# Column-softmax products with the operands exchanged, and a transpose by DMA behind them

## The chip, the cores and the metric

The kernel runs on one core of a Trainium2 chip. A core has five instruction streams that work side by side and meet only through semaphores: TensorE (PE, matrix products, with a separate weight-load part PEld), VectorE (DVE), ScalarE (ACT), GpSimd (POOL) and SyncE (SP), which in this kernel issues DMAs and computes nothing. Each stream takes its instructions strictly in the order in which the program lists them; an instruction that waits holds back all that stand behind it on the same stream. The metric is the device time of one execution in microseconds (us); lower is better.

## The reference, cut to what matters

```python
B, H, S, Ns, D = (8, 8, 512, 32, 64)
scores = scale * x @ state.T                 # per (batch, head): 512 x 32
a = softmax(scores, -1);   xread = a @ state # row softmax, result 512 x 64
scores2 = scale * state @ x.T                # per (batch, head): 32 x 512
a2 = softmax(scores2, -1); sread = a2 @ x    # column softmax, result 32 x 64
attn = concatenate([xread, sread], axis=2)   # per head 544 rows of 64
t = attn.transpose(0, 2, 1, 3).reshape(B * 544, 512)
h = maximum(t @ w_in, 0)                     # 512 -> 2048
out = (s * h * h + b) @ w_out                # 2048 -> 512
```

The change concerns `sread`: for each batch and head, the 32 x 512 weights `a2` times the 512 x 64 block of `x`. The 8 x 32 rows of `sread` (all heads side by side, 512 columns) are the last 256 tokens that go through the two layers.

## The kernel before, in words

The order of all the work is written out by hand in the list `ORDER` (lines 15 to 79). Each word names a piece and its arguments; the loop at line 785 calls the pieces one after another, and each engine's stream is the order of these calls. Batches are handled in the order 0 to 7 for the main work, while the `sread` work of a batch comes later and in the order 3, 4, 5, 2, 6, 0, 7, 1.

For one batch `b` the `sread` work is this chain. `nm`, `E2` and `a2` make the column softmax on ACT and DVE (tile `a2`, 128 partitions = 4 heads x 32 states, two groups `g` of 4 heads, 512 tokens). `tr` (line 446) turns it by one DMA issued from SP into `a2T`, with tokens on the partitions: 8 blocks of 128 x 128. `V` (line 450) multiplies it on PE with `xn`, the batch's `x` with tokens on the partitions, and `srd` (line 470) copies the result `vps` from PSUM into `srdT` on ACT.

In `V` of the kernel before, `xn` (64 columns, the head's D) is the operand that is loaded into the array, and 32 columns of `a2T` move through it. The result has D on the partitions, 64 for each of two heads, so the array is used as two column tiles of 64. For each `k` (four pairs of heads) and each of `SCH` = 4 chunks of tokens there are two matmuls: 32 per batch. The result is already in the layout that the first layer wants, and `srd` writes it with a step: `srdT` is `[P, NK, Ns, B]` and `srdT[:, :, :, b]` touches every eighth fp16 element, 16 bytes apart.

`lsr` (line 544) is the first layer for the `sread` tokens: 16 calls of four matmuls each, all of which read `srdT` as the moving operand with 256 columns (32 states x 8 batches). For each `k` those 256 elements lie next to one another. They need `srdT` of all eight batches; the first call (`lsr.14`) stands near the end of `ORDER`.

The main work of a batch: `M` makes the product of states and `w_in`, `Mc` copies it from PSUM, `l` (line 526) is the first layer, `s` squares, `S` makes sums of blocks, and `P` (line 645) is the second layer by seven block products. The products go into PSUM banks X, Y and W; DVE takes a bank out with `ev` (line 660) into the output tiles `osx0` and `osx1`. Bank W is read out twice, by `ev.b.W1` after its first block product and by `ev.b.W2` after its second, which adds on top; so the second product into W (`P.b.10` and `P.b.11`) may only start when `ev.b.W1` has read the bank. `put.b.i.rr` (line 668) stores 128 rows of `osx{i}` by two DMAs, from SP for all batches but the last.

`osx0` and `osx1` have one buffer each (`bufs=1`, line 614). So the first `ev` of the next batch into the tile waits until all four store DMAs of the batch before have landed: `ev.b.X1` waits for the stores of `put.(b-1).0.*`, `ev.b.W1` for those of `put.(b-1).1.*`.

The SP stream therefore carries, mixed in one order: the transposes `tr` (line 448) and `xt` (line 316, 16 blocks of 128 x 128, `x` with D on the partitions), the copies of line 275, and the stores.

Of the kernel before, what the change touches and what calls it, by code (L numbers as in the profile page):

```python
# [11 lines left out]
FP16 = mybir.dt.float16  # L12
# [70 lines left out]
def kernel(  # L83
# [12 lines left out]
    nc = tc.nc  # L96
# [4 lines left out]
    B, H, S, D = x.shape  # L101
    Ns = state.shape[2]
    DM = H * D
    DF = moe_w_in.shape[1]
    P = 128
    NK = DM // P
    NKF = DF // P
    NG = H // 4
    SCH = S // P
# [10 lines left out]
    konst = ctx.enter_context(tc.tile_pool(name="konst", bufs=1))  # L120
    wpool = ctx.enter_context(tc.tile_pool(name="wpool", bufs=1))
    xpool = ctx.enter_context(tc.tile_pool(name="xpool", bufs=4))
    apool = ctx.enter_context(tc.tile_pool(name="apool", bufs=1))
# [11 lines left out]
    def two_banks(name, dtype=FP32, own=False):  # L135

        pool, tag = (ps_t, "pt") if own else (ps_a, "pa")
        return pool.tile([P, 2, 2048 // mybir.dt.size(dtype)], dtype, name=name, tag=tag)

    def mm(out, lhsT, rhs, start=True, stop=True, tp=None, is_transpose=None, skip=False):  # L140
        skip = skip or out.offset * mybir.dt.size(out.dtype) >= 2048
        return nc.tensor.matmul(  # L142
            out, lhsT, rhs, start=start, stop=stop, tile_position=tp,
            is_transpose=is_transpose, skip_group_check=skip,
        )
# [27 lines left out]
    ones16 = konst.tile([P, 512], FP16, name="ones16")  # L173
    c16 = konst.tile([P, DM], FP16, name="c16")
    bias_bc = konst.tile([P, DM], FP32, name="bias_bc")
    srdT = konst.tile([P, NK, Ns, B], FP16, name="srdT")
    w_in16 = [wpool.tile([P, NK, 512], FP16, name=f"w_in16_{j}") for j in range(NJ)]
    w_out16 = wpool.tile([P, NKF, DM], FP16, name="w_out16")

# [58 lines left out]
    def w_in_f(k, f):  # L238
        return w_in16[f // 4][:, k, P * (f % 4) : P * (f % 4) + P]
# [41 lines left out]
    at = [dict() for _ in range(B)]  # L281

    def sm(b, key, shape, dtype, pool=None, bufs=None):
        if key not in at[b]:
            at[b][key] = (pool or smpool).tile(
                shape, dtype, name=f"{key}_{b}", tag=key, bufs=bufs
            )
        return at[b][key]
# [161 lines left out]
    def at_V(own, *bs):  # L450

        pair = two_banks(f"vps_{bs[0]}", own=own)
        for v, b in enumerate(bs):
            vps = pair[:, v, : NK * Ns].rearrange("p (k n) -> p k n", n=Ns)
            a2T, xn = at[b]["a2T"], xn_t[b]
            for k in range(NK):
                for i in range(SCH):
                    for g in range(NG):
                        hp = k ^ 2 * g
                        mm(  # L460
                            vps[D * g : D * g + D, k, :],
                            xn[:, 4 * g + k, i, :],
                            a2T[:, SCH * g + i, Ns * hp : Ns * hp + Ns],
                            start=(i == 0),
                            stop=(i == SCH - 1),
                            tp=(0, D * g),
                        )
            at[b]["vps"] = vps

    def at_srd(b):  # L470
        nc.scalar.copy(srdT[:, :, :, b], at[b]["vps"])

    def at_M(b, j, own):
        M = sm(b, "M", [P, NG, DF], FP16, mpool)
# [26 lines left out]
    def in_turn(shape, name, tag, n):  # L501
        k = turns[tag] = turns.get(tag, -1) + 1
        return rpool.tile(shape, FP16, name=name, tag=f"{tag}{k % n}", bufs=1)

    def layer1(tag, f, terms, ntok):
        hps = ps_h.tile([P, ntok], FP32, name=f"hps_{tag}_{f}", tag="ph")
        for i, (lhsT, rhs) in enumerate(terms):
            to = hps if len(rhs.shape) == 2 else hps.rearrange("p (c q) -> p c q", c=2)
            nc.tensor.matmul(to, lhsT, rhs, start=(i == 0), stop=(i == len(terms) - 1))  # L509
        q, i = f // 4, f % 4  # L510
        if (tag, q) not in R_t:
            R_t[tag, q] = in_turn([P, 4, ntok], f"r_{tag}_{q}", "r", 3)
        nc.scalar.activation(R_t[tag, q][:, i], hps, AF.Relu)  # L513
# [12 lines left out]
    def layer1_x(b, f):  # L526
        M, A = at[b]["M"], at[b]["A"]
        layer1(b, f, [(M[:, g, P * f : P * f + P], of_head(b, A, g)) for g in range(NG)], S)
# [13 lines left out]
        squared(e, new_G(b, S)[:, f : f + 2, HALF * p : HALF * p + HALF], R_t.pop((b, f, p)))  # L542

    def layer1_sr(f):
        layer1("sr", f, [(w_in_f(k, f), srdT[:, k].rearrange("p n b -> p (n b)")) for k in range(NK)], B * Ns)

    ops_t, visits = {}, {}

# [215 lines left out]
    def evict_sr(i, n, bank, plus, last):  # L764
# [12 lines left out]
        "sb": spread_scalars, "xT": at_xT, "xt": at_xt, "cs": copy_states, "T": at_T, "keep": at_keep, "U": at_U, "mu": at_mu, "D": at_D,  # L777
        "E1": at_E1, "z": at_z, "At": at_At, "A": at_A, "nm": at_nm, "nms": at_nms, "E2": at_E2, "a2": at_a2,
        "tr": at_tr, "V": at_V, "srd": at_srd, "M": at_M, "Mc": at_Mc,
        "lh": layer1_half, "sh": square_half, "l": layer1_x, "s": square, "lsr": layer1_sr,  # L780
        "ssr": lambda f, n, e: square("sr", f, n, e), "L": layer2, "out": out_x, "cps": bias_sum, "c": bias_c16,
        "bias": bias_all, "wsum": weight_sum, "S": act_sum, "P": product, "ev": evict, "put": put,
# [36 lines left out]
```

## Time and profile before

| what | value |
|---|---|
| median of 3 runs (lowest, highest) | 211.52 us (211.32, 211.72) |
| the profiled execution: its own time | 211.45 us |
| its span on the core | 209.7 us |
| PE busy | 200.1 us, 95% of the span |
| DVE / ACT / POOL busy | 179.0 us (85%) / 169.1 us (81%) / 47.4 us (23%) |
| granted TensorE clock, mean | 0.984 |
| HBM read / written | 20.48 MB / 8.91 MB |

The profiled execution lies inside the spread of the timed runs. Its time is 1.75 us above its span; that part lies outside what the trace shows.

How to read the rows in this document. A timeline row gives the start in us, the duration in us, the engine, the line of the kernel, the operation, what is written from what, the shape, and how many instructions were merged (`x32`). For PE the shape ahead of the result's is the loaded operand: `128*64` is 128 rows and 64 columns of the array. `SPq` is SP's queue: a row there is the time that the issue of a DMA takes, and the transfer itself goes on behind it. A group row of one line or one tile gives the least, the median and the greatest duration in ns and the first and last start; "DMA to landing" is the time from the start of an issue to the data's arrival. A row of stretches gives for each engine its busy time (and the instructions), then the granted clock, the DMA share and GB/s.

### The profile page before, as it was taken

The page shows a single profiled execution, that of the slowest core. Times are in us where ns is not written, and L with a number is a line of the kernel's source. Part 1 is how long each engine was busy: PE and PEld are TensorE (multiplying, and loading weights), DVE is VectorE, ACT ScalarE, POOL GpSimd, SP SyncE. Part 2 cuts the span into 40 slices and gives each one's busy share as a digit, 9 for nine tenths or more (in the row PEclk, how much of TensorE's full clock was granted, in tenths as well). Part 3 has the DMA queues.
Part 4 walks back from the last instruction along what each step waited for, and adds up shares of the span by engine and source line. Part 5 has one row for each costly group of instructions (what it writes and reads, how often), then busy time and mean ns, then how long its engine had stood idle before and what let it go on. Part 6 is the DMA issues. An engine that isn't in the chain of part 4 may idle for free.

```text
span 209.7 us, 4807 instructions
## 1 busy us (share of the span) xinstructions
PE 200.1 (95%) x1939; PEld 131.4 (63%) x1939; DVE 179.0 (85%) x276; ACT 169.1 (81%) x275; POOL 47.4 (23%) x63
## 2 busy tenths in 40 slices
PE   7498998999999999999999999999999999999992
PEld 2134343344576757676677677766777677888881
DVE  2998999799999899999999999999995984476571
ACT  4589999999999999989999677997989688634500
POOL 8553360524074009300470007100000000000000
PEclk9859999999999999999999999999999999999999
DMA  6999999699448539959799353719004910440055
GB/s 152 179 207 207 195 205 204 110 144 165 99 79 96 107 78 183 147 86 195 163 128 189 74 118 65 100 42 199 12 0 88 187 31 0 96 107 0 5 149 152
DMA packets 42475, 24.87 MB, mean 119 GB/s; under 512 B 24532, under 2 KB 37588, under 8 KB 42452
## 3 DMA queue, kind: packets, MB, share of 16 engines
q0 software_dynamic: 15408, 9.90, 34.0%
q1 hardware_dynamic: 25760, 13.70, 31.3%
q10 hardware_dynamic: 1284, 0.95, 1.6%
q8 instruction: 15, 0.25, 0.5%
q14 instruction: 8, 0.07, 0.1%
HBM read 20.48 MB, written 8.91 MB: 140 GB/s over the span
## 4 chain that ended last, share of the span: by engine, by line
PE 86%; DVE 6%; DMA 3%; ACT 1%; POOL 1%; issue 1%; DVEq 0%; POOLq 0%
PE opf_X L142 24%; PE hps L509 23%; PE opf_W L142 12%; PE opf_Y L142 6%; PE ops L558 5%; PE mps L142 4%; DMA w_in<-in_moe_w_in_dram 3%; PE hps_sr L509 3%; PE vps L142 2%; PE ops_sr_X L142 2%; DVE M L157 1%; PE hph L142 1%; ACT M L157 1%; PE dps L733 1%; PE ops_sr_W L142 1%; DVE g L519 1%
## 5 line engine op out<-in xcount | busy, mean ns | idle before, releaser
L513 ACT ACTIVATE r<-hps 128x512 f16<-128x512 f32 x120 | 69.2, 619 | 11.1 <-PE hps L509 9.0
L142 PEld LDWEIGHTS <-g 128*128 128x128 f16 x672 | 65.2, 98 | 17.8 <-issue 1.5
L509 PE MATMUL hps<-A,M 128*128 128x512 f16 x240 | 64.8, 379 | 0.4 <-ACT M L157 0.3
L517 ACT ACTIVATE g<-r 128x1024 f16<-128x1024 f16 (+1 forms) x37 | 46.1, 1262 | 0.0
L509 PEld LDWEIGHTS <-M 128*128 128x128 f16 x240 | 22.0, 98 | 19.7 <-issue 5.2
L142 PE MATMUL opf_X<-w_T,g 128*128 128x256 f16 x224 | 28.4, 273 | 0.0
L634 DVE TENSOR_TENSOR g<-g 128x1024 f16<-128x1024 f16 (+1 forms) x36 | 25.5, 709 | 0.6
L157 ACT CAST M<-mps 128x1024 f16<-128x1024 f32 x21 | 21.2, 1032 | 2.5 <-PE mps L142 2.5
L196 POOL DMA_DIRECT2D xn<-in_x_dram x32 | 18.5, 584 | 4.2 <-DMA w_in<-in_moe_w_in_dram 1.8
L634 POOL TENSOR_TENSOR g<-g 128x1024 f16<-128x1024 f16 x4 | 8.5, 2125 | 46.1 <-DVE g L634 32.4
L664 DVE SCALAR_TENSOR_TENSOR osx<-opf_X,sb_bc,bias_bc 128x512 f32<-128x512 f32 x21 | 15.5, 737 | 1.5 <-PE opf_X L142 1.4
L558 PE MATMUL ops<-w_out,g 128*128 128x512 f16 x64 | 16.0, 379 | 0.0
L142 PE MATMUL opf_X<-w_out,g 128*128 128x256 f16 x112 | 14.4, 273 | 0.0
L142 PE MATMUL opf_Y<-w_out,g 128*128 128x256 f16 x112 | 14.3, 273 | 0.0
L142 PE MATMUL opf_W<-w_T,g 128*128 128x256 f16 x112 | 14.2, 273 | 0.0
L142 PE MATMUL opf_X<-w_T,S 128*128 128x256 f16 x112 | 14.2, 272 | 0.0
L142 PE MATMUL opf_W<-w_out,g 128*128 128x256 f16 x112 | 13.9, 273 | 0.0
L142 PE MATMUL mps<-w_in,stT 64*32 64x512 f16 x256 | 12.4, 411 | 1.4 <-DMA w_in<-in_moe_w_in_dram 1.4
L157 DVE CAST M<-mps 128x1024 f16<-128x1024 f32 x11 | 13.2, 1215 | 0.4 <-PE mps L142 0.4
L513 ACT ACTIVATE r_sr<-hps_sr 128x256 f16<-128x256 f32 x16 | 6.1, 382 | 9.2 <-PE hps_sr L509 8.5
L142 PEld LDWEIGHTS <-S 128*128 128x128 f16 x112 | 11.0, 98 | 2.9 <-issue 0.2
L634 DVE TENSOR_TENSOR S<-g 128x1024 f16<-128x1024 f16 x14 | 9.5, 682 | 2.3 <-ACT g L517 2.2
(98 smaller groups left out, 272.9 us busy)
## 6 DMA issues: line engine op xcount, KB each, us to landing
out_dram<-osx SPq DMA_DIRECT2D x52, 128.0 KB, 2.4
xn<-in_x_dram POOLq DMA_DIRECT2D x32, 128.0 KB, 5.3
w_in<-in_moe_w_in_dram POOLq DMA_DIRECT2D x8, 256.0 KB, 9.4
w_out<-in_moe_w_out_dram POOLq DMA_DIRECT2D x4, 512.0 KB, 13.2
xh<-in_x_dram POOLq DMA_DIRECT2D x4, 256.0 KB, 11.3
out_dram<-osb SPq DMA_DIRECT2D x16, 64.0 KB, 1.8
xf<-in_x_dram SPq DMA_DIRECT2D x2, 256.0 KB, 3.6
out_dram<-osx ACTq DMA_DIRECT2D x4, 128.0 KB, 2.9
```

Of the source, the lines that this page charges most:

```text
L142: return nc.tensor.matmul(out, lhsT, rhs, start=start, stop=stop, tile_position=tp, is_transpose=is_transpose, skip_group_check=skip,)
L157: (engine.copy if engine is nc.scalar else engine.tensor_copy)(out, in_)
L196: nc.gpsimd.dma_start(out=xn_t[b][32 * jh : 32 * jh + 32].rearrange("t h c d -> t h (c d)"), in_=x[b].rearrange("h (t jh c) d -> jh t h (c ...
L509: nc.tensor.matmul(to, lhsT, rhs, start=(i == 0), stop=(i == len(terms) - 1))
L513: nc.scalar.activation(R_t[tag, q][:, i], hps, AF.Relu)
L517: nc.scalar.activation(g, r, AF.Square)
L519: e.tensor_mul(g, r, r)
L558: nc.tensor.matmul(ops_t[tag, rr], G_t[tag][:, f, P * rr : P * rr + P], w_out_f(f), start=(v == 1 and f == 4 * q), stop=(v == NKF // 4 and ...
L634: e.tensor_tensor(out, x, y, op)
L664: nc.vector.scalar_tensor_tensor(out, fast(b, name[0]), s_bc, out if plus else bias, ALU.mult, ALU.add)
L733: nc.tensor.matmul(dps, ones16[:, :P], ones16, start=True, stop=True)
```

## The change

Three things change.

`V`: the operands are exchanged. The 32 columns of `a2T` are loaded and 64 columns of `xn` move. The result has the states on the partitions, 32 for each of four heads, so the array is used as four column tiles of 32. There are still 32 matmuls per batch; the loop runs over `g`, then the chunks, then the four tiles `k`.

`srd`: ACT copies the 128 x 128 result into a new small tile `sr16` (two buffers), with neighbouring elements, and a DMA issued from SP transposes that into `srdT`. This is one more DMA per batch on SP's stream, of one 128 x 128 block, eight in all, and each waits for ACT's copy. The words of `ORDER` are the same; the new DMA stands where the word `srd.b` stands.

`srdT` becomes `[P, B, P]`: for each batch 128 columns, which are four groups `k` of 32 states. `lsr` reads `srdT[:, :, Ns*k : Ns*k+Ns]` as 32 states x 8 batches, the batch running fastest: neighbours in the moving operand are now 128 elements, 256 bytes, apart. The order of the 256 tokens in the result is the same as before.

```diff
-    srdT = konst.tile([P, NK, Ns, B], FP16, name="srdT")
+    srdT = konst.tile([P, B, P], FP16, name="srdT")
...
-            vps = pair[:, v, : NK * Ns].rearrange("p (k n) -> p k n", n=Ns)
+            vps = pair[:, v, :P]
             a2T, xn = at[b]["a2T"], xn_t[b]
-            for k in range(NK):
+            for g in range(NG):
                 for i in range(SCH):
-                    for g in range(NG):
+                    for k in range(NK):
                         hp = k ^ 2 * g
                         mm(
-                            vps[D * g : D * g + D, k, :],
+                            vps[Ns * k : Ns * k + Ns, D * g : D * g + D],
+                            a2T[:, SCH * g + i, Ns * hp : Ns * hp + Ns],
                             xn[:, 4 * g + k, i, :],
-                            a2T[:, SCH * g + i, Ns * hp : Ns * hp + Ns],
                             start=(i == 0),
                             stop=(i == SCH - 1),
-                            tp=(0, D * g),
+                            tp=(0, Ns * k),
                         )
...
     def at_srd(b):
-        nc.scalar.copy(srdT[:, :, :, b], at[b]["vps"])
+        sr16 = sm(b, "sr16", [P, P], FP16, apool, 2)
+        nc.scalar.copy(sr16, at[b]["vps"])
+        nc.sync.dma_start_transpose(out=srdT[:, b : b + 1, :], in_=sr16)
...
-            to = hps if len(rhs.shape) == 2 else hps.rearrange("p (c q) -> p c q", c=2)
+            to = hps if len(rhs.shape) == 2 else hps.rearrange("p (c q) -> p c q", c=rhs.shape[1])
...
-        layer1("sr", f, [(w_in_f(k, f), srdT[:, k].rearrange("p n b -> p (n b)")) for k in range(NK)], B * Ns)
+        layer1("sr", f, [(w_in_f(k, f), srdT[:, :, Ns * k : Ns * k + Ns].rearrange("p b n -> p n b")) for k in range(NK)], B * Ns)
```

## The prediction

> **What bounds the kernel now.** I read the page first (span, busy shares, chain), then the stretches, then the timeline around the eight products, then SP's queue.
>
> ```profile
> span 209.7 us, 4807 instructions
> PE 200.1 (95%) x1939; PEld 131.4 (63%) x1939; DVE 179.0 (85%) x276; ACT 169.1 (81%) x275; POOL 47.4 (23%) x63
> PE 86%; DVE 6%; DMA 3%; ACT 1%; POOL 1%; issue 1%; DVEq 0%; POOLq 0%
> 85.00:95.00 10.00, 10.00 (x114) 6.78 (x112) 9.96 (x15) 9.04 (x13) 0.68 (x2) 1.00 0.85 115
> 95.00:105.00 10.00, 10.00 (x106) 6.36 (x103) 9.57 (x17) 9.69 (x18) 2.74 (x3) 1.00 0.90 183
> 105.00:125.00 20.00, 20.00 (x240) 14.49 (x240) 19.30 (x30) 16.78 (x29) 3.72 (x7) 1.00 0.81 128
> 125.00:150.00 25.00, 25.00 (x226) 17.34 (x224) 23.86 (x33) 22.10 (x34) 4.38 (x5) 1.00 0.51 91
> ```
>
> The chain that ends last is PE for 86% of the span, and in the middle of the run PE never rests. So PE work taken away there is worth its full time, and so is every us that PE is made to wait. DVE stands right behind: between 85 and 150 us it is idle for only 0.04 + 0.43 + 0.70 + 1.14 = 2.3 us. SP has no busy time, but its order matters, and there the new DMAs go in.
>
> **The change part by part.** First the products on PE.
>
> ```profile
> 91.72 0.68 PE L142 MATMUL vps<-a2T,xn 128*64 128x32 f16 x32
> 92.33 1.04 PE L509 MATMUL hps<-A,M 128*128 128x512 f16 x4
> 167.55 1.19 PE L142 MATMUL vps<-a2T,xn 128*64 128x32 f16 x64
> 168.67 0.39 PE L142 MATMUL opf_X<-w_T,g 128*128 128x256 f16 x2
> 36.55 1.05 PE L142 MATMUL cps<-w_out,ones 128*32 128x512 f16 x16
> ```
>
> One batch keeps PE for 92.33 - 91.72 = 0.61 us, two batches for 168.67 - 167.55 = 1.12: the second 32 matmuls cost 0.51, or 0.032 for each pair of 64-column tiles, and about 0.10 is the change of tiling. The kernel has a four-tile case too: 16 matmuls of `cps` with 32 columns loaded and 512 moving take 1.05, as long as four full-width ones (1.04). So four narrow tiles move their columns at the same time. In the new form a group of four loads 4 x 32 columns and moves 64. I price a group like a pair now, 0.032, since the larger of the two operands is 64 columns in both: 8 groups, 0.26 per batch, 0.25 less. The bounds: no gain if loading were per matmul (0.51), and 0.15 if it were by moved columns alone. Of the eight batches, three visits count in full (batch 3; 5 with 2; 6 with 0): 5 x 0.255 = 1.28 us off. Batch 4 sits ahead of a wait described below and gains nothing, 7 and 1 are counted there.
>
> Next, ACT's copy.
>
> ```profile
> L471 ACT CAST srdT<-vps x8: 726/736/782, 68.1 to 173.3; 128x128 f16<-128x128 f32 x8
> L513 ACT ACTIVATE r_sr<-hps_sr x16: 374/383/384, 178.2 to 196.1; 128x256 f16<-128x256 f32 x16
> 95.07 0.74 ACT L471 CAST srdT<-vps 128x128 f16<-128x128 f32 x1
> 166.41 0.73 ACT L471 CAST srdT<-vps 128x128 f16<-128x128 f32 x1
> 173.29 0.73 ACT L471 CAST srdT<-vps 128x128 f16<-128x128 f32 x1
> ```
>
> The copy of 128 elements at 16-byte steps takes 0.74, while an activation of 256 neighbouring ones takes 0.38. With neighbouring writes I take 0.27 (the bounds: 0.2 and 0.38), 8 x 0.47 = 3.8 us less on ACT. I count it at nothing in the sum, because ACT is not on the path; it brings the copy's end forward, and there I use 0.27.
>
> Then SP, the main part. The built program shows where the eight transposes stand: behind `put.1.1.1` and ahead of `put.1.1.0` (batch 4); between `put.5.0.1` and `put.5.0.0` (6), with `tr.1` behind; then 7 and 1 ahead of all four stores of `put.5.1`. The other four (3, 5, 2, 0) stand where SP waits anyway for something later than the copy, and cost nothing. Each transpose waits for ACT's copy, and SP waits with it.
>
> ```profile
> 79.47 2.49 SPq L673 DMA_DIRECT2D out_dram<-osx  x4
> 160.40 2.48 SPq L673 DMA_DIRECT2D out_dram<-osx  x4
> 163.34 1.25 SPq L448 DMA_TRANSPOSE a2T<-a  x1
> 164.69 2.49 SPq L673 DMA_DIRECT2D out_dram<-osx  x4
> L448 SPq DMA_TRANSPOSE a2T<-a x8: 1236/1254/1360, 57.3 to 163.3; - x8
> DMA to landing us min/median/max: 3.1/3.1/3.4
> L316 SPq DMA_TRANSPOSE xT<-xn x5: 1343/1970/3323, 38.3 to 110.6; - x5
> DMA to landing us min/median/max: 4.3/4.7/5.8
> DMA to landing us min/median/max: 2.3/2.4/3.8
> ```
>
> The landings are, in order, those of line 448, of line 316 and of the stores of line 673. A transpose of 8 blocks is issued in 1.24 us at least, one of 16 in 1.34: 0.013 per block, so one block takes about 1.14 to issue. Landing takes 3.1 and 4.7, 0.2 per block: about 1.7 for one. The bounds are the issue of a store (2.49 / 4 = 0.62) and that of 8 blocks (1.25). All three places below are followed from the copy's end in before's times.
>
> ```profile
> 90.65 0.75 DVE L664 SCALAR_TENSOR_TENSOR osx<-opf_W,sb_bc,bias_bc 128x512 f32<-128x512 f32 x1
> 93.20 1.91 PE L142 MATMUL opf_W<-w_out,g 128*128 128x256 f16 x16
> 166.98 0.74 DVE L664 SCALAR_TENSOR_TENSOR osx<-opf_X,sb_bc,bias_bc 128x512 f32<-128x512 f32 x1
> 174.21 0.75 DVE L664 SCALAR_TENSOR_TENSOR osx<-opf_W,sb_bc,bias_bc 128x512 f32<-128x512 f32 x1 [0.99 <-PE opf_W L142]
> 176.66 1.04 PE L142 MATMUL opf_W<-w_out,g 128*128 128x256 f16 x8
> 177.54 0.60 PE L509 MATMUL hps_sr<-srdT,w_in 128*128 128x256 f16 x4
> ```
>
> *Batch 4.* The stores of `put.1.1.0` are the last two of the row at 79.47. In the changed kernel they wait for the copy that starts at 95.07: copy done 95.34, transpose issued 96.48, second store issued 97.10, landed 99.50. `ev.2.W1` (90.65) needs that tile free, so DVE stands for 99.50 - 90.65 = 8.85 us. It ends at 100.25, and the second product into bank W (93.20) may only then begin: PE stands for 7.05. ACT's copy does not hang on either, so there is no way round. DVE has 2.3 us of rest until 150 to catch up, PE has none; I take 8.0, bounds 7.05 and 8.85.
>
> *Batch 6.* Copy done 166.41 + 0.27 = 166.68, transpose issued 167.82, two stores 169.06; only then is `tr.1` issued, which was issued at 163.34 before, and it lands at 172.16. The product of batch 1 wanted it at about 167.8. With 0.26 for the product and 0.1 for the tiling PE goes on at 172.53 instead of 168.67: 3.9 us. DVE's `ev.6.X1` (166.98) waits for the same two stores, landed at 170.84, which this covers.
>
> *Batches 7 and 1.* Shifted by 3.9, the copy of batch 1 ends at 177.46, its transpose is issued at 178.60, the fourth store at 180.46 and lands at 182.86. `ev.6.W1` (174.21 before, 178.1 shifted) ends at 183.6, and the second product into W (176.66, shifted 180.56) waits 3.0 us. `lsr.14`, behind it, then starts at 184.4; the last transpose has landed by 180.6 even at 3.1, so `lsr` waits for nothing new. `sr16` has two buffers, so a copy waits for the transpose two before it, which in all cases is long through.
>
> With a plain store's 0.62 for each issue, the last two become 3.4 and 2.5.
>
> What PE's rest does to its clock has one example:
>
> ```profile
> 5.00:10.00 5.00, 2.75 (x40) 0.96 (x38) 4.57 (x10) 2.85 (x6) 3.05 (x5) 0.93 1.18 176
> 9.31:16.13 6.82, 5.82 (x44) 1.93 (x43) 6.58 (x13) 5.31 (x7) 4.16 (x6) 0.50 1.20 206
> ```
>
> After a loosely filled stretch the granted clock is 0.50 for 6.82 us, which is 3.4 us of PE time lost. Two new rests (7.05, 4.4) are long; a loss of up to 3.4 behind each, partly under DVE's lag in the first: I take 1.7 in all, bounds 0 and 6.8. The Trainium skill (TensorE: Matmul & The Clock Gate, Part 1) gives half the clock after an idle window of about 3.4 us; this trace agrees on the half and on the length, as 6.82 is two such windows. By that rule the third rest, 3.0, would cost nothing.
>
> Last, the moving operand of `lsr`.
>
> ```profile
> 181.03 1.04 PE L509 MATMUL hps_sr<-srdT,w_in 128*128 128x256 f16 x8
> L509 PE MATMUL hps_sr<-srdT,w_in x64: 272/273/273, 177.5 to 195.8; 128*128 128x256 f16 x64
> ```
>
> Eight take 1.04, of which the last one's own 0.273 overlaps the next: (1.04 - 0.273) / 7 = 0.11 each. No row shows a moving operand read at 256-byte steps. Below, it costs nothing more (0.11, the same engine reading neighbours). Above, ACT's copy at 16-byte steps pays (736 - 270) / 128 = 3.6 ns more per element, 256 x 3.6 = 0.93 us per matmul, 60 us in all. That row is a write by another engine; PE's own is nearer, yet a step that leaves ACT's line of neighbours clearly isn't free here. I take one further pass of the 256 columns: 64 x 0.109 = 7.0 us, all on the path, since ACT waits for PE in that stage. The Trainium skill (SBUF — State Buffer, Specifications (TRN2)) speaks against the change: SBUF lines are 16 bytes, and full bandwidth needs at least two hits per line; every element here lies in a line of its own. By it, half the rate, estimated 7 us; no run here shows it for PE.
>
> Sum against the profiled execution (211.45, span 209.7, 1.75 outside the span; the median of the runs is 211.52): 211.45 - 1.28 + 8.0 + 3.9 + 3.0 + 1.7 + 7.0 = 233.8 us.
>
> **The rivals.** *B, the queue alone:* the strided read is free. Everything else as above: 226.8. For it speaks that PE's rows show no slow moving operand at all; against it, ACT's copy.
>
> *C, the read alone:* the waits on SP fall into slack. 211.45 - 8 x 0.255 + 7.0 = 216.4. Against it: the stores at 79.47 are 15.6 us ahead of the copy they would wait for, and 90.65 leaves DVE nothing to do meanwhile.
>
> *D, faster:* both hidden, PE keeps the shorter products: 211.45 - 2.04 = 209.4. Its one mechanism is the shorter stay of 32 matmuls on a path that is PE. It decides only if SP gets past each new transpose before the next reader; at batch 6 that needs 163.34 to move by less than 167.8 - 163.34 - 3.1 = 1.4 us, and the copy alone is 3 us later.
>
> *E, worse:* the read costs over two passes, or the clock halves behind every rest: above 240.
>
> **How the numbers follow.** Forecast 0.50, B 0.33, C 0.06, D 0.05, E 0.06. Forecast and B hold 0.83. With the least of each term (7.05, 3.4, 2.5, no clock loss, free read) B is 223.1; with the greatest (8.85, 3.9, 3.0, 6.8, 7.0) the forecast is 239.7. The range is 222.5 to 240.5; the forecast's own is 229 to 240. A measurement of this kernel tells 0.2% (0.4 us) from no change: faster 0.05 (D), within it 0.01, slower 0.94.
>
> **What would show it.** Right: `vps` of 32 in about 0.36; the copy at 0.27; SP in a transpose of line 473 until after ACT's copy of batch 4, then two stores; DVE without work for some 9 us near 91 and PE for 7 near 93; a second PE rest at batch 1's product and a third ahead of `lsr`; `hps_sr` some 0.22 apart; the clock at 0.5 behind the first rest. Wrong: stores of batch 1 that land before the copy of batch 4 (the queue does not hold), or `hps_sr` still 0.11 apart (B).

## The result, and the profile after

The changed kernel takes 255.84 us (median of 6 runs, 254.18 to 259.58); the kernel before, run beside it, takes 211.62 (211.32 to 211.97). The ratio is 1.207, with a 95% interval of 1.202 to 1.212; it leaves out the longest run, which is over 1.5% above the shortest. The forecast was 233.8 us with a range of 222.5 to 240.5: the direction was right, the size was not, by 22 us. The profiled execution is the longest of the six (259.58, span 257.8), some 4 us above the median. What sets it apart is not shown, since only this execution has a trace: the mean granted clocks of the six go from 0.910 to 0.939, the two highest belong to two of the three shortest runs, but the lowest to the run of 257.72 us and not to the longest.

The page of the changed kernel; the columns of the groups are total busy time, mean ns, and the idle time ahead of them with its releaser:

```profile
span 257.8 us, 4826 instructions
PE 230.4 (89%) x1939; PEld 135.9 (53%) x1939; DVE 180.4 (70%) x276; ACT 166.0 (64%) x275; POOL 46.9 (18%) x63
PE 74%; DVE 10%; DMA 6%; ACT 3%; issue 2%; SPq 2%; POOL 1%; DVEq 0%; POOLq 0%
L515 ACT ACTIVATE r_sr<-hps_sr 128x256 f16<-128x256 f32 x16 | 6.1, 383 | 39.3 <-PE hps_sr L511 39.3
L511 PE MATMUL hps_sr<-srdT,w_in 128*128 128x256 f16 x64 | 29.3, 608 | 0.0
L666 DVE SCALAR_TENSOR_TENSOR osx<-opf_W,sb_bc,bias_bc 128x512 f32<-128x512 f32 x7 | 5.2, 746 | 18.1 <-DMA out_dram<-osx 15.9
```

Two readings. DVE and DMA take 10% and 6% of the chain now: `opf_W`'s evictions stand idle for 18.1 us, 15.9 of them for the stores of `osx`. And PE's busy time has grown by 30 us: one `hps_sr` takes 608 ns instead of 273, and ACT waits 39.3 us for them.

The timeline of PE in the changed kernel (a bracket gives the rest ahead of the row and who ended it):

```profile
92.96 0.42 PE L142 MATMUL vps<-xn,a2T 128*32 128x64 f16 x32
93.31 1.04 PE L511 MATMUL hps<-A,M 128*128 128x512 f16 x4
...
101.76 3.57 PE L142 MATMUL opf_W<-w_out,g 128*128 128x256 f16 x16 [7.41 <-DVE osx L666]
...
182.54 0.62 PE L142 MATMUL vps<-xn,a2T 128*32 128x64 f16 x32 [4.45 <-DMA a2T<-a]
...
196.72 1.03 PE L142 MATMUL opf_W<-w_out,g 128*128 128x256 f16 x8 [3.40 <-DVE osx L666]
...
197.59 1.89 PE L511 MATMUL hps_sr<-srdT,w_in 128*128 128x256 f16 x4
...
203.73 1.05 PE L142 MATMUL opf_X<-w_T,g 128*128 128x256 f16 x8
204.62 3.62 PE L511 MATMUL hps_sr<-srdT,w_in 128*128 128x256 f16 x8
208.07 1.87 PE L142 MATMUL opf_X<-w_out,g 128*128 128x256 f16 x8
```

The three rests stand at the three places of the prediction, with their releasers: 7.41, 4.45 and 3.40 us. The product itself is shorter (93.31 - 92.96 = 0.35 for a batch). The new thing is the last rows: eight `hps_sr` take 3.62 us instead of 1.04, that is (3.62 - 0.61) / 7 = 0.43 from start to start instead of 0.11; and behind them eight plain matmuls take 1.87 instead of 1.05, half clock, though PE has not rested.

SP's queue in the changed kernel, around the first two places:

```profile
80.44 1.20 SPq L675 DMA_DIRECT2D out_dram<-osx  x2
96.62 1.12 SPq L473 DMA_TRANSPOSE srdT<-sr  x1
97.78 1.23 SPq L675 DMA_DIRECT2D out_dram<-osx  x2
...
178.00 1.22 SPq L675 DMA_DIRECT2D out_dram<-osx  x2
179.34 1.29 SPq L448 DMA_TRANSPOSE a2T<-a  x1
```

SP issues two of batch 1's last four stores at 80.44, then nothing for 15 us until ACT's copy of batch 4 is there, then the transpose, then the other two stores. DVE's row answers it:

```profile
100.95 0.75 DVE L666 SCALAR_TENSOR_TENSOR osx<-opf_W,sb_bc,bias_bc 128x512 f32<-128x512 f32 x1 [8.96 <-DMA out_dram<-osx]
```

The tile `sr16` of the changed kernel (the profile leaves numbers at the end of a name out and writes `sr`), by least, median and greatest duration in ns:

```profile
L472 ACT CAST sr<-vps x8: 260/266/318, 69.7 to 189.9; 128x128 f16<-128x128 f32 x8
L473 SPq DMA_TRANSPOSE srdT<-sr x8: 1107/1122/1927, 72.3 to 190.2; - x8
DMA to landing us min/median/max: 2.2/2.6/6.5
```

And three stretches of the changed kernel, the clock in the third column from the end: behind the first rest, behind the second, and the stage of `lsr`.

```profile
101.76:105.70 3.94, 3.94 (x18) 2.69 (x18) 3.90 (x7) 0.00 (x0) 0.00 (x0) 0.50 0.50 93
182.54:187.70 5.16, 5.16 (x51) 3.31 (x52) 2.85 (x6) 0.60 (x1) 0.00 (x0) 0.50 0.01 3
201.40:242.50 41.10, 41.10 (x156) 18.78 (x155) 11.33 (x18) 8.38 (x19) 0.00 (x0) 0.83 0.12 26
```

This gives the account of the profiled execution, 48.1 us of span in all. Up to the first `hps_sr` it is 197.59 - 177.54 = 20.05 us later: rests 7.41 + 4.45 + 3.40 and one of 0.43 make 15.7; work at half clock behind the first two 3.94 / 2 + 5.16 / 2 = 4.6; the shorter products, all eight since the rests are counted from their ends, -1.8 (two single batches at 0.61 - 0.35 and three pairs at 1.12 - 0.69); and 1.6 is the loosely filled start of the run, which differs between executions (the product `T_None` stands at 34.23 instead of 32.64). That is 20.1. From the first `hps_sr` to the end it takes 60.2 instead of 32.2 us, 28.0 more. Of this 64 x (0.432 - 0.109) = 20.7 is the slow read, and 7.3 is left for the half clock in that stage, about 1 of it behind the third rest (from 197.9 to 201.3).

### The profile page after: what moved, and what is told of

It reads as the page before. It is cut to its first block, busy times and chain, and to the rows that moved or that the text cites. A ratio compares the mean times of both kernels' runs of the same rounds, so it can differ in the third digit from the quotient of the medians.

```text
span 257.8 us, 4826 instructions
## 1 busy us (share of the span) xinstructions
PE 230.4 (89%) x1939; PEld 135.9 (53%) x1939; DVE 180.4 (70%) x276; ACT 166.0 (64%) x275; POOL 46.9 (18%) x63
## 4 chain that ended last, share of the span: by engine, by line
PE 74%; DVE 10%; DMA 6%; ACT 3%; issue 2%; SPq 2%; POOL 1%; DVEq 0%; POOLq 0%
PE opf_X L142 18%; PE hps L511 17%; PE hps_sr L511 11%; PE opf_W L142 11%; PE opf_Y L142 4%; PE ops L560 4%; PE mps L142 3%; DMA w_in<-in_moe_w_in_dram 3%; DVE osx L666 2%; DMA out_dram<-osx 2%; DVE At L390 1%; SPq L675 1%; PE ops_sr_X L142 1%; ACT r L515 1%; DMA a2T<-a 1%
## 5 line engine op out<-in xcount | busy, mean ns | idle before, releaser
L142 PEld LDWEIGHTS <-g 128*128 128x128 f16 x672 | 69.6, 104 | 38.9 <-issue 19.3
L515 ACT ACTIVATE r<-hps 128x512 f16<-128x512 f32 x120 | 67.9, 609 | 30.3 <-PE hps L511 29.5
L515 ACT ACTIVATE r_sr<-hps_sr 128x256 f16<-128x256 f32 x16 | 6.1, 383 | 39.3 <-PE hps_sr L511 39.3
L142 PE MATMUL opf_X<-w_T,g 128*128 128x256 f16 x224 | 31.2, 289 | 0.0
L511 PE MATMUL hps_sr<-srdT,w_in 128*128 128x256 f16 x64 | 29.3, 608 | 0.0
L142 PE MATMUL opf_W<-w_out,g 128*128 128x256 f16 x112 | 18.0, 323 | 10.8 <-DVE osx L666 10.8
L666 DVE SCALAR_TENSOR_TENSOR osx<-opf_W,sb_bc,bias_bc 128x512 f32<-128x512 f32 x7 | 5.2, 746 | 18.1 <-DMA out_dram<-osx 15.9
L142 PE MATMUL opf_X<-w_T,S 128*128 128x256 f16 x112 | 15.8, 293 | 0.4 <-DVE osx L666 0.4
L142 PE MATMUL opf_Y<-w_out,g 128*128 128x256 f16 x112 | 15.2, 283 | 0.0
L142 PE MATMUL opf_W<-w_T,g 128*128 128x256 f16 x112 | 15.1, 283 | 0.0
L511 PEld LDWEIGHTS <-w_in 128*128 128x128 f16 x64 | 7.5, 117 | 14.4 <-issue 13.8
## 6 DMA issues: line engine op xcount, KB each, us to landing
xh<-in_x_dram POOLq DMA_DIRECT2D x4, 256.0 KB, 11.3
```

The source lines that it names most:

```text
L142: return nc.tensor.matmul(out, lhsT, rhs, start=start, stop=stop, tile_position=tp, is_transpose=is_transpose, skip_group_check=skip,)
L666: nc.vector.scalar_tensor_tensor(out, fast(b, name[0]), s_bc, out if plus else bias, ALU.mult, ALU.add)
```

## The experiments

Each is told as an edit against the changed kernel or the kernel before. The order of the words in `ORDER` is given in words, since a diff of its lines says little.

### The read alone, and the three mends

**The read alone** (against before; operands and copy engine as before, no DMA):

```diff
-    srdT = konst.tile([P, NK, Ns, B], FP16, name="srdT")
+    srdT = konst.tile([P, B, P], FP16, name="srdT")
...
-        nc.scalar.copy(srdT[:, :, :, b], at[b]["vps"])
+        nc.scalar.copy(srdT[:, b].rearrange("p (k n) -> p k n", n=Ns), at[b]["vps"])
...
-        layer1("sr", f, [(w_in_f(k, f), srdT[:, k].rearrange("p n b -> p (n b)")) for k in range(NK)], B * Ns)
+        layer1("sr", f, [(w_in_f(k, f), srdT[:, :, Ns * k : Ns * k + Ns].rearrange("p b n -> p n b")) for k in range(NK)], B * Ns)
```

> Before's products, with the copy written to neighbouring addresses and the first layer of the sread rows (lsr) reading its moving operand at 256-byte steps as in the changed kernel; no transposing DMA at all. Theory 1 (what the changed kernel's trace suggests): each of the 64 matmuls now starts 0.434 us after the last instead of 0.109, 64 x 0.325 = 20.8 us, and if the clock windows at half speed in that stage hang on the read, some 3 to 5 us more: 232 to 238. Theory 2 (as predicted, one further pass): 211.5 + 7.0 = 218.5, and the 0.434 would come from something else, such as the DMA transposes still under way. Theory 3 (the read is free): 211 to 212.

Measured: 236.66 us (median of four runs, 232.24 to 238.89). Theory 1 holds. The tile `hps_sr` in the execution of 238.89 us, the one with a trace:

```profile
L509 PE MATMUL hps_sr<-srdT,w_in x64: 592/610/618, 178.8 to 222.8; 128*128 128x256 f16 x64
```

610 ns, as in the changed kernel, with no DMA transpose anywhere. From the first to the last `hps_sr` it takes 44.0 us, against 195.8 - 177.5 = 18.3 before: 25.7 more, 20.7 for the reads and some 5 for the clock, which in this stage falls to half four times. The four runs take 232.24, 235.87, 237.45 and 238.89 us at mean granted clocks of 0.992, 0.978, 0.963 and 0.941: the time goes with the clock. The shortest is 232.24 - 211.48 = 20.8 us above the kernel before, run beside it, which is about the price of the reads (20.7), and its clock leaves room for some 3.7 us at half clock in the whole run (0.008 x 230.4 / 0.5). So the slow read is paid in every run, the half clock in most.

**Runs of 32** (against the changed kernel; the stores at the end follow the new order of the rows, in blocks of 32):

```diff
-        layer1("sr", f, [(w_in_f(k, f), srdT[:, :, Ns * k : Ns * k + Ns].rearrange("p b n -> p n b")) for k in range(NK)], B * Ns)
+        layer1("sr", f, [(w_in_f(k, f), srdT[:, :, Ns * k : Ns * k + Ns]) for k in range(NK)], B * Ns)
...
-    out_sr = out_BSn[:, S:ST, :].rearrange("b (r t) n -> r t b n", r=2)
+    out_sr = out_BSn[:, S:ST, :].rearrange("(r b) t n -> r b t n", r=2)
...
-            (nc.sync if i else nc.scalar).dma_start(out_sr[i][:, :, sl], out[:, sl])
+            for b in range(4):
+                (nc.scalar if b % 2 else nc.sync).dma_start(out_sr[i][b][:, sl], out[Ns * b : Ns * b + Ns, sl])
```

> The changed kernel, but the sread tokens are ordered batch by batch, so that lsr reads runs of 32 neighbours; the last stores go out in blocks of 32 rows. The transposes stay where they are on SP. Theory 1 (queue and read are two separate costs): hps_sr start 0.11 us apart, the three rests of PE stay (about 7.4, 4.4 and 3 us), 226 to 229, which is the rival of the queue alone (226.8). Theory 2 (the read is the whole cost, the rests are taken up elsewhere): 211 to 216. Theory 3 (runs of 32 are as slow as single elements): as the changed kernel, about 255.

Measured: 233.0 us, ratio 1.102 (1.096 to 1.107), above the numbers of theory 1, though its two costs are separate as it says. The read is plain again, the three rests stay (7.39, 4.47, 3.39), and it is 6 us more than the forecast for the queue alone (226.8). The clock tells why. Three stretches that begin at the end of each rest:

```profile
100.25:106.00 5.75, 5.75 (x36) 2.90 (x35) 5.68 (x10) 1.29 (x2) 0.00 (x0) 0.50 0.71 129
181.84:184.70 2.86, 2.86 (x42) 1.94 (x43) 2.00 (x4) 0.00 (x0) 0.00 (x0) 0.52 0.03 6
194.85:198.90 4.05, 4.05 (x23) 2.92 (x23) 1.37 (x3) 1.24 (x2) 0.00 (x0) 0.58 0.00 0
```

The work lost is 5.75 x 0.50 + 2.86 x 0.48 + 4.05 x 0.42 = 6.0 us, where 1.7 was taken. A further 1.7 is the tail: from DVE's last start to the end of the span it is 231.2 - 225.5 = 5.7 us, before 209.7 - 205.7 = 4.0.

**SP's order alone.** The stores of `put.1.1.0` go ahead of batch 4's transpose, `put.5.0.0` and `tr.1` ahead of batch 6's, `put.5.1.*` ahead of batch 7's; the read stays at 256-byte steps.

> The changed kernel with only the order of SP's queue mended: the last two stores of batch 1's put ahead of batch 4's transpose, the stores and the transpose of a that stood behind batch 6's transpose ahead of it, the stores of put.5.1 ahead of batch 7's. The read at 256-byte steps stays. Theory 1: the three rests go (16 us) with the half-clock stretches behind them (3 to 7 us), the read stays: 232 to 238. Theory 2 (the transposes themselves cost the time, wherever they stand): no more than 3 us less than the changed kernel, 252 to 255.

Measured: 237.6 us, ratio 1.123 (1.115 to 1.131). Theory 1: 18.2 us come off. But PE has a new rest of 2.46 us, which the next run explains.

**Both mended**: the two edits above together.

> Both mended: the order of SP's queue, and lsr reading runs of 32 neighbours. Theory 1 (queue order and read are all that the change costs): PE keeps the shorter products, 8 x 0.255 = 2.0 us less than before, less a little for the finer stores at the end: 209.0 to 210.5. Theory 2 (the transposes or the copies in between cost something of their own): 212 to 216.

Measured: 215.25 us, ratio 1.017 (1.012 to 1.022): inside theory 2's numbers, but not for its reason. SP before, then SP and PE in this kernel:

```profile
92.19 1.25 SPq L448 DMA_TRANSPOSE a2T<-a  x1
93.67 1.97 SPq L316 DMA_TRANSPOSE xT<-xn  x1
```

```profile
95.17 1.12 SPq L473 DMA_TRANSPOSE srdT<-sr  x1
96.40 1.24 SPq L448 DMA_TRANSPOSE a2T<-a  x1
97.86 3.16 SPq L316 DMA_TRANSPOSE xT<-xn  x1
```

```profile
103.13 0.63 PE L142 MATMUL T<-xT,stC 64*32 64x256 f16 x16 [2.54 <-DMA xT<-xn]
```

It is not the transposing itself that costs this, but its place once more, as the next run shows. Before, the transposes of `a` for batch 5 and of `x` for batch 6 were issued at 92.19 and 93.67; behind the new transpose, which waits for ACT's copy, they start 4.2 us later, and the `T` product of batch 6 waits for `xT`. In the changed kernel the same two are late too, but there PE's rest of 7.41 us covers it. The prediction named only the stores as queued behind that transpose.

**That place mended too**: the transpose gets a word of its own in `ORDER` (`sx`), and batch 4's goes behind the two transposes, batch 6's behind `tr.1`; `sr16` gets three buffers instead of two.

```diff
-        nc.sync.dma_start_transpose(out=srdT[:, b : b + 1, :], in_=sr16)
+    def at_sx(b):
+        nc.sync.dma_start_transpose(out=srdT[:, b : b + 1, :], in_=at[b]["sr16"])
```

> Both mended as in the last experiment but with batch 4's transpose put behind the two transposes (of a for batch 5, of x for batch 6) which it held up there: SP issues each new transpose only where nothing wanted stands behind it. lsr reads runs of 32 neighbours; the last stores still go out in 16 blocks. Theory 1 (the 2.5 us rest of PE for xT and the half clock behind it were SP's order once more): 4 us less than 215.25, 210.5 to 212, of which 1.6 is the tail of finer stores. Theory 2 (the DMA transposes in themselves slow the others on their way): PE still rests for xT, 213 to 216.

Measured: 211.98 us, ratio 1.002 (0.999 to 1.005). PE's rest for `xT` is gone: theory 1. The whole change is now a draw; PE reaches `lsr` at 176.2 instead of 177.5, and loses that 1.3 us and a little more in the tail, which is 1.7 longer.

### Each place of the queue by itself

Both start from the kernel of 233.0 us (runs of 32, finer stores, all eight transposes as in the change); `sr16` has three buffers in both. First batch 4's transpose alone moved behind all that it held up:

> The kernel of 233.0 us (the change with lsr reading runs of 32) with one move alone: batch 4's transpose goes behind the stores, the transpose of a and that of x which it held up. Theory 1 (the batch 4 place is worth its rest and the half clock behind it): 7.39 us of rest and half of the 5.75 us at half clock that PE works behind it, 10.3 in all: 222 to 224. Theory 2 (the rest is handed on to the next places, as DVE and SP come earlier to them): 226 to 230.

Measured: 223.44 us, 9.6 less. Then the other two places alone:

> The same kernel of 233.0 us with the other two places alone mended (the transposes of batches 6, 7 and 1 behind the transpose of a for batch 1 and the stores of put.5). Theory 1: rests of 4.47 and 3.39 us, and half of about 2.8 and 3.9 us at half clock, 11.2 in all: 221 to 223. Theory 2 (one of the two rests stays, since the other one covered it): 224 to 228.

Measured: 222.04 us, 11.0 less. The two gains sum to 20.6; mending all three gave 233.0 - 211.98 = 21.0. Both lie inside theory 1's numbers. So the places are independent to within 0.4 us, which is less than the runs of one kernel differ by, the rests are not handed on, and each is worth about its rest plus the half clock behind it (10.3 and 11.2 by the expectations).

### The price of the step

Two kernels from before, in which the four matmuls of each `lsr` read differently stored groups: `srdTa` to `srdTd` at steps of 4, 8, 16 and 32 bytes, and `srdTe` to `srdTh` as single elements at 64 and 128 bytes, pairs at 128, runs of four at 256. The edit for the first:

```diff
-        nc.scalar.copy(srdT[:, :, :, b], at[b]["vps"])
+        vps = at[b]["vps"]
+        nc.scalar.copy(srd4[0][:, :, b], vps[:, 0].rearrange("p (h l) -> p h l", l=2))
+        nc.scalar.copy(srd4[1][:, :, b], vps[:, 1].rearrange("p (h l) -> p h l", l=4))
...
```

> Before's kernel with the result stored four ways, one per group of weights, so that the 256 moved elements of lsr's four matmuls are read at steps of 4, 8, 16 and 32 bytes (tiles srdTa to srdTd; ACT makes four small copies per batch instead of one). Read from start to start of the single matmuls; the total time only rises a little. Theory 1 (each element that lies in a line of its own costs a fixed 1.7 ns): 0.109 at 4 and 8 bytes, and 0.43 at 16 and 32. Theory 2 (the price grows with the step): 0.2 or less at 4 bytes, rising to 0.43 only beyond 32 bytes. Theory 3 (anything but neighbours is slow): 0.43 for all four.

> The same with single elements at steps of 64 and 128 bytes (tiles srdTe and srdTf), pairs of neighbours at steps of 128 bytes (srdTg), and runs of four neighbours at steps of 256 bytes (srdTh). Theory 1 (a price per line of 16 bytes touched): 0.43 for the two of single elements; the pairs 0.22, the runs of four 0.11. Theory 2 (the price grows with the step): more at 128 bytes than at 64, and pairs no cheaper than single elements at the same step.

Each was measured once, at 224.32 and 223.04 us, 12.6 and 11.3 above before; the rows below give 64 x (0.31 - 0.11) = 12.8 and 64 x (0.30 - 0.11) = 12.2. Timelines of PE, first of the one, then of the other; the start of the next row less that of a row is its price:

```profile
185.91 0.28 PE L518 MATMUL hps_sr<-srdTa,w_in 128*128 128x256 f16 x1
186.03 0.39 PE L518 MATMUL hps_sr<-srdTb,w_in 128*128 128x256 f16 x1
186.24 0.62 PE L518 MATMUL hps_sr<-srdTc,w_in 128*128 128x256 f16 x1
186.68 0.64 PE L518 MATMUL hps_sr<-srdTd,w_in 128*128 128x256 f16 x1
187.14 0.30 PE L518 MATMUL hps_sr<-srdTa,w_in 128*128 128x256 f16 x1
```

```profile
185.24 0.59 PE L518 MATMUL hps_sr<-srdTe,w_in 128*128 128x256 f16 x1
185.66 0.61 PE L518 MATMUL hps_sr<-srdTf,w_in 128*128 128x256 f16 x1
186.09 0.40 PE L518 MATMUL hps_sr<-srdTg,w_in 128*128 128x256 f16 x1
186.31 0.30 PE L518 MATMUL hps_sr<-srdTh,w_in 128*128 128x256 f16 x1
186.44 0.59 PE L518 MATMUL hps_sr<-srdTe,w_in 128*128 128x256 f16 x1
```

| how the 256 fp16 are read | elements in 16 bytes | us from start to start |
|---|---|---|
| neighbours (before) | 8 | 0.109 |
| step 4 bytes | 4 | 0.12 |
| runs of four, 256 bytes apart | 4 | 0.13 |
| step 8 bytes | 2 | 0.21 |
| pairs, 128 bytes apart | 2 | 0.22 |
| step 16 / 32 bytes | 1 | 0.44 / 0.46 |
| step 64 / 128 / 256 bytes (the last in the changed kernel) | 1 | 0.42 / 0.43 / 0.43 |

Every row up to two elements in 16 bytes fits a price of 1.6 to 1.8 ns (0.43 us / 256 = 1.7) per 16 bytes touched; with four the time comes near the plain rate. The distance between the lines hardly matters. Theory 1 of both holds in kind, but in the first it put 8-byte steps at 0.109, which is wrong. The Trainium skill (SBUF — State Buffer, Specifications (TRN2)), which the prediction leaned on, asks for two hits per line for the full rate; here two give half of it, and four come to within a tenth to a fifth of it. In these two kernels the clock in the `lsr` stage stays whole, for instance over all 31 us of the first:

```profile
177.40:208.50 31.10, 31.10 (x170) 17.27 (x169) 12.20 (x20) 9.72 (x21) 0.00 (x0) 1.00 0.16 35
```

There a mean `hps_sr` takes (0.12 + 0.21 + 0.44 + 0.46) / 4 = 0.31 us, where it takes 0.43 the clock falls. So the read at single elements can cost twice: its own time, and a clock that behaves as if PE were partly resting while it waits for its operand. The fall comes in the traced executions of all three kernels that have the read (the shortest run of the read alone had little of it or none), and in none of those without, but for what a rest just ahead of `lsr` leaves behind. How the clock counts is not shown by an experiment; the last section has a count of the records that fits the reads and the rests alike.

### Where to put the order of the tokens

The mended kernel of 211.98 us has its rows in another order, which costs it the tail. Three ways to get rid of that.

**One store per half again**, with four blocks of rows as its slowest step:

```diff
-            for b in range(4):
-                (nc.scalar if b % 2 else nc.sync).dma_start(out_sr[i][b][:, sl], out[Ns * b : Ns * b + Ns, sl])
+            (nc.sync if i else nc.scalar).dma_start(out_sr[i][:, :, sl], out[:, sl])
```

> The version of 211.98 us (order of SP mended at all three places, lsr reading runs of 32 neighbours) with its last stores in one DMA per half again, as before. Theory 1 (the 1.6 us at the end were the 16 finer stores): 209.8 to 210.8, faster than before by 0.4 to 0.8%; PE's first lsr product stood at 176.2 against 177.5 in before, 1.3 us earlier. Theory 2 (the end is late for another reason, such as the rows' addresses): 211.5 to 212.2.

Measured: 216.43 us, ratio 1.022 (1.019 to 1.025). Both theories are wrong: it is worse by 4.5. DVE's last step starts at 204.39, 1.3 us before that of before, and the span ends at 214.2. One us of the tail in this kernel, and one of before (clock, DMA share, GB/s at the end):

```profile
208.00:209.00 1.00, 0.00 (x0) 0.00 (x0) 0.00 (x0) 0.00 (x0) 0.00 (x0) 0.50 0.26 84
```

```profile
207.00:208.00 1.00, 0.00 (x0) 0.00 (x0) 0.00 (x0) 0.00 (x0) 0.00 (x0) 1.00 0.95 296
```

A share of 0.26 means that about a quarter of the DMA engines' time is used, instead of nearly all. The Trainium skill (DMA: Bandwidth & Descriptors, Rules for kernel authors) says that the slowest step's size bounds the number of engines, so four here; the share of 0.26 agrees. Before has 16 steps there.

**Before's products with the same layout and stores, no DMA:**

> Before's products and no DMA at all, with the copy written to neighbouring addresses by batch and lsr reading runs of 32 neighbours; the last stores one per half. ACT saves 8 x 0.47 us. Theory 1 (ACT is off the path, runs of 32 cost PE nothing): as before, 211.0 to 212.0. Theory 2 (ACT's time was on the path, or the read of runs costs): 209 or 213 and more.

Measured: 217.71 us, ratio 1.028 (1.025 to 1.032): theory 2's numbers, but by neither of its reasons. It is again the tail: DVE's last step starts at 205.32, 0.4 us earlier than before, and the span ends at 215.8. So the total says nothing on ACT's copy, and the start of the last step says that its 3.8 us are worth about 0.4.

**PE writes PSUM with a step** (32 bytes), stores as in before:

```diff
+            to = hps.rearrange("p (n b) -> p b n", b=B) if tag == "sr" else ...
```

> The same order on SP, with the last stores as before: lsr reads runs of 32 neighbours and writes its 256 results into PSUM at steps of 8 elements (32 bytes), so that the tokens come out in before's order. Theory 1 (the step on the result's side is free): PE keeps the shorter products, 8 x 0.255 = 2.0 us, and nothing else is left of the change: 209.0 to 210.3. Theory 2 (the result's step costs what the operand's did): hps_sr 0.43 apart again, 230 to 236.

Measured: 217.02 us, ratio 1.024 (1.020 to 1.027), between the two theories. A row of PE's timeline in this kernel:

```profile
180.89 1.89 PE L513 MATMUL hps_sr<-srdT,w_in 128*128 128x256 f16 x8
```

(1.89 - 0.42) / 7 = 0.21 each: writing at a step costs a factor of two, 64 x 0.10 = 6.4 us, where reading costs four. The Trainium skill (PSUM — Partial Sum Buffer, Specifications (TRN2)) says without a figure that a non-contiguous pattern slows a matmul; the trace agrees and gives the factor.

**ACT reads PSUM with a step** (128 bytes) and writes neighbours, stores as in before:

```diff
-        nc.scalar.activation(R_t[tag, q][:, i], hps, AF.Relu)
+        if tag == "sr":
+            nc.scalar.activation(
+                R_t[tag, q][:, i].rearrange("p (n b) -> p n b", b=B), hps.rearrange("p (b n) -> p n b", b=B), AF.Relu
+            )
...
```

> The version of 211.98 us with the token order turned back at another place: PE reads runs of 32 and writes PSUM in the same order, ACT's activation r_sr reads its 256 results from PSUM at steps of 32 elements (128 bytes) and writes neighbours; the last stores stand as in before. Theory 1 (ACT reads PSUM at steps for nothing): 0.38 us for each of the 16, and PE's shorter products show as the prediction had them: 210.0 to 210.8, faster than before by 0.5 to 0.8%. Theory 2 (reading costs what the write at 16-byte steps did, 3.6 ns per element): 0.92 us more for each, 15 us on ACT against some 9 us that it waits there now: 216 to 220.

Measured: 210.28 us against 211.71, ratio 0.993 (0.990 to 0.995): faster than both kernels, and theory 1. ACT's row in this kernel:

```profile
L518 ACT ACTIVATE r_sr<-hps_sr x16: 374/383/383, 177.1 to 194.9; 128x256 f16<-128x256 f32 x16
```

383 ns, as without the step: free. The whole change gains 1.4 us after all (0.5% to 1.0%), about 0.4 of which may be ACT's shorter copy, once the transposes stand where nothing waits behind them and no engine pays for the order of the tokens.

## Why the prediction was wrong, point by point

- *The moving operand of `lsr`* is the step that failed: "I take one further pass of the 256 columns: 64 x 0.109 = 7.0 us". It measured 20.7 (0.43 instead of 0.11, three further passes). That the read costs PE time, and where, was right; its size was not, and it is 13.7 us of the miss. The price was taken for one further pass without a row, though the prediction itself had an upper bound of 60 from ACT's copy, and the range did not take that bound in: its upper end used the same 7.0. ACT's row, set aside as a write by another engine, touches 16 bytes per element too, and paid 3.6 ns for it where PE pays 1.7 in all; whether for the same reason is not shown. The last rival, "the read costs over two passes, or the clock halves behind every rest", at 0.06, is what happened, in both its halves.
- *The clock* is the second mis-sized term: 1.7 was taken, bounds 0 and 6.8. Behind the rests it was 4.6 up to `lsr` in the changed kernel, with about 1 more behind the third, which was held to cost nothing, and 6.0 with the plain read, near the upper bound. That the clock would fall inside the `lsr` stage, where PE never rests, was not thought of; in the traced executions it is 2 to 7 us (7.3 in the profiled execution of the changed kernel; in the kernel with SP's order alone `lsr` runs 220.1 - 178.8 = 41.3 us, 23.0 longer than before, so 2.3 beside the reads).
- *Batch 4*: 8.0 foreseen, rest 7.41, worth 9.6 with its clock. Stores, DVE's wait and the product that waits are as told. *Batch 6*: 3.9 foreseen, 4.45. *Batches 7 and 1*: 3.0 foreseen, 3.40. The issue of a transpose, 1.14 foreseen, took 1.12; its landing, estimated at 1.7, took 2.2 at least and 2.6 in the median, and lies in these differences.
- *The products*: 0.36 for a batch alone foreseen with the change of tiling, 0.35 measured. For two in turn it would have been 0.62, but they take 0.69, so 0.10 is not the change of tiling alone, and all eight save 1.8 us where 2.0 were foreseen. The lower bound of 0.15 does not come out of the prediction's rows: 512 moved columns at 0.109 per 256 are 0.22. *ACT's copy*: 0.27 foreseen, 266 ns measured, and rightly counted at nothing.
- *What is queued behind* batch 4's transpose: the transposes of `a` and `x` behind it were left out. In the changed kernel the longer rest hides them; without it they cost 215.25 - 211.98 = 3.3 us.
- *A smaller slip*: the low ends of the last two places, 3.4 and 2.5, are worked out with a store's 0.62 for the issue; batch 4's, 7.05, is not and would have been 6.5.

In sum, the forecast falls short of the profiled execution by 259.58 - 233.8 = 25.8 us: 13.7 for the read, 4.6 + 7.3 - 1.7 = 10.2 for the clock, 0.8 for the rests and 1.6 for the start of the run, less 0.5 for the products. In medians, the two costs add up: mending three places of the queue takes 255.84 - 237.6 = 18.2 us off with the slow read and 233.0 - 215.25 = 17.8 with the plain one.

## What to carry to other kernels

Ask of every operand that changes its layout how many elements the reader finds in 16 bytes, and look for the engine on which the step is free: here it cost PE's read (256-byte steps) a factor of four, PE's write into PSUM (32-byte steps) a factor of two, and ACT's read from PSUM (128-byte steps) nothing. A DMA whose data comes late belongs in its queue behind everything that is ready earlier; list what stands behind it up to the next thing that waits as long, not only its first neighbour. And when a price has no row, let the range reach to the bound that you worked out yourself.

## What the runs showed of the hardware

*Price per 16 bytes.* About 1.7 ns of PE for each 16 bytes of SBUF that its moving operand of 256 fp16 columns touches, with one or two elements in them, at steps from 8 to 256 bytes, and the same at a granted clock of 0.5: at full clock a `hps_sr` of the changed kernel starts every 0.43 us, and in the half clock around 240 four of them took 242.37 - 240.63 = 1.74, 0.435 each, while a plain matmul ahead of them took (240.63 - 238.95) / 8 = 0.21 instead of 0.11.

```profile
238.95 1.89 PE L142 MATMUL opf_X<-w_T,S 128*128 128x256 f16 x8
240.63 1.92 PE L511 MATMUL hps_sr<-srdT,w_in 128*128 128x256 f16 x4
242.37 3.52 PE L142 MATMUL opf_W<-w_out,g 128*128 128x256 f16 x16
```

*Rests and the clock.* Rests of 0.38 to 0.45 us never lowered it, nor did one of 2.08 us early in the changed kernel. Those of 4.43 us and more always did. In between it went both ways: two stretches that follow a rest of 2.46 us (SP's order alone) and one of 2.54 (both mended),

```profile
102.81:106.20 3.39, 3.39 (x38) 2.31 (x39) 3.36 (x6) 1.64 (x4) 2.17 (x2) 1.00 0.97 204
```

```profile
103.13:106.20 3.07, 3.07 (x26) 1.65 (x27) 3.04 (x4) 0.60 (x1) 1.70 (x1) 0.50 0.99 213
```

and one that follows a rest of 3.39 us (batch 4's place mended alone), where the changed kernel ran at half clock from 197.9 to 201.3, soon behind a rest of 3.40:

```profile
185.66:189.70 4.04, 4.04 (x38) 3.62 (x38) 2.10 (x3) 1.68 (x4) 0.00 (x0) 1.00 0.00 0
```

The Trainium skill (TensorE: Matmul & The Clock Gate, Part 1) has a window of about 3.4 us that runs freely, so that it matters where in it a rest lies; the pairs agree with that, but a rest of 2.54 us that costs half the clock is shorter than the idle window it gives.

*A count that fits.* From 30 us into the run to PE's last matmul, every stretch at half clock in these traces lasts 3.41, 6.83 or 10.24 us, and within a trace they all begin and end whole multiples of 3.41 us apart. So a run can be cut into windows of 3.41 us on that grid. Count in each what PE loses: its rest, and what each `hps_sr` takes beyond the plain 0.11 us. In the 15 traces there are 79 windows at full clock that lose over 0.3 us. The 19 that lose 2.06 us or more are all followed by half clock, and the 60 that lose 2.04 or less never. The rest of 2.46 us from 100.35 to 102.81 has 1.68 in one window (101.13 to 104.54), that of 2.54 us from 100.59 to 103.13 has 2.19 (99.37 to 102.78): hence the different rows. The same count gives the fall in `lsr`: some windows of the three kernels with the slow read lose 2.06 to 2.55 us, while no window of the two kernels with four kinds of read loses over 1.64. This is a count over records, not an experiment. Taken as an estimate, a rest under 2.05 us costs no clock, one over 4.1 us always does, since one window then holds half of it or more, and in between it is luck; both cases belong into the range.
